# Sigmoid attention and mixture of depths on one core: sums moved from GpSimd to VectorE, small transfers moved to GpSimd, and a new order at the end

## The chip, the cores and the metric

The kernel runs on one core of a Trainium2 chip. The metric is device time in microseconds (us), the median of the runs of one kernel. The kernel before takes 510.37 us (three runs, 508.68 to 512.42).

A core has five engines, each with an instruction stream of its own: TensorE (PE in the profile; its weight loads are PEld), VectorE (DVE), ScalarE (ACT), GpSimd (POOL) and SyncE (SP), which here only issues transfers. Each works strictly in its program's order: what waits at the head of a stream holds up all that stands behind it. Transfers between HBM and the on-chip memory (SBUF) run on DMA engines. They are issued by SyncE or by GpSimd, each of which has a queue of its own. Products land in PSUM, in eight banks.

## The reference

```python
# attention: q, k, v are (8 batches, 12 heads, 448 tokens, 64), float32
scores = q @ k^T / 8 - log(448)
attn   = sigmoid(scores)
x      = attn @ v, heads side by side: (8, 448, 768)
# mixture of depths, per batch b
s      = x[b] @ w_gate                       # one score per token
top    = the 128 tokens with the largest s
h      = relu(x[b, top] @ w1)                # w1: 768 x 1024
ye     = h @ w2                              # w2: 1024 x 768
out[b] = x[b]; out[b, top] += sigmoid(s[top]) * ye
```

## The kernel before

**Attention, by stage.** A stage `s` (0 to 11) handles two groups of four heads, in seven units `n`. A unit (`unit`, L269 and L277) multiplies a block of keys with all queries and puts the sigmoid on ScalarE. The product with the values (`values`, L304) runs in four steps: step 0 at the end of its own stage, steps 1 to 3 in the first three units of the next. `take` (L319) then turns the result into rows per token on VectorE, and `gates` (L327, L330) adds up gate scores from them. Keys and queries come in by token (`load`, L100), and VectorE turns them (`turn`, L244 to L251): for stage s+1 after unit 5 of stage s, and the second half early in stage s+1. The values come by `load_v` (L119, L121) after unit 3.

**Routing, by batch.** A batch is complete after one and a half stages. `store` (L336) writes its rows to DRAM, `gate` (L348 to L363) makes the scores, `spread` (L370) brings them to all partitions by way of DRAM (L358), `rank` (L378, L381) counts how many tokens score higher, and `place` (L389 to L394) carries the ranks through DRAM into a tile `spot`. `choose` (L406 to L426) picks from it the token of each rank and its score, puts the sigmoid on that score (L421, ScalarE) and gathers the 128 rows `xe` (GpSimd, L426). `copy_out` (L339) copies all rows to the output, and `scatter` (L567, GpSimd) writes the chosen rows over them at the end.

The small transfers of this chain (scores, rep, ranks, spot) are issued by GpSimd for batches 0 and 1 (scores and rep for 7 also), and by SyncE for the others. On SyncE they stand among the large ones, and rep waits there until scores has landed, spot until ranks has.

**The two matrix products of the chosen rows** work on pairs `p` of batches, with a scheme of Strassen's kind: instead of eight products of half-size blocks there are seven, of sums of blocks. So there are sums on three sides:

- Sums of the weights, four for each matrix, made once: `load_weights` (L135 to L167). It loads four quarters of a matrix (L152), makes four 128x1536 sums on GpSimd (L166) and stores each in DRAM (L157). It is called for matrix 1 after unit 5 of stage 0, and for matrix 2 after unit 5 of stage 1. Later `lend` (L177) brings a sum back into tiles that the attention has just freed, shortly before its product.
- Sums of the turned rows: `turn_rows` transposes `xe` on TensorE (L448), ScalarE and VectorE copy it out of PSUM (L451 to L454), and three sums of 128x384 follow (L457), a fourth in `last_row` (L467). They run on VectorE for pairs 0 and 3 and on GpSimd for pairs 1 and 2.
- Sums of the hidden rows: `first` makes the seven products with matrix 1 (L484). `first_sums` adds their results on VectorE (L497) and applies relu on ScalarE (L500). After product 3 come four more sums, of hidden rows with each other: on GpSimd for pairs 0 to 2 (L532), and on VectorE for pair 3 (L522 to L527). `second` makes the seven products with matrix 2 (L546), and `second_sums` multiplies by the gate and adds to `xe` (L557).

**What sets the order.** It is written out by hand; nothing reorders it. `WORK` (L577) says after which unit of which stage each product stands, `LENT` (L589) which sums are lent in which stage, and `routed` and `gap` where the routing steps go. In `do` (L601), the sums of first product 7 are held until those of the next product have been issued. After stage 11, `rest` (L667) lists the remaining work: the last batches' routing, the pair 2 and then the pair 3.

Of the kernel before, what the change touches and what calls it, by code (L numbers as in the profile page):

```python
# [17 lines left out]
def kernel(  # L18
# [124 lines left out]
    def load_weights(m):  # L143
        n = KH if m == 1 else FH
        w = (w1_sb, w2_sb)[m - 1]
        held = [(0, 0), (0, 1), (1, 1)] if m == 1 else [(0, 0), (1, 0), (1, 1)]
        left = (1, 0) if m == 1 else (0, 1)
        room = moe.tile([P, 7 * FH * P], F32, name="hidden")
        a, b = room[:, :QW], room[:, QW:2 * QW]
        c = moe.tile([P, 6 * KH * P], F32, name="rows_t")[:, :QW]  # L150
        for dst, at in [(a, left)] + [(w[:, x], held[x]) for x in (2, 0, 1)]:
            nc.sync.dma_start(out=dst.rearrange("p (t c) -> p t c", t=n), in_=quarter(m, *at))  # L152
        w00, wx, w11 = [w[:, x] for x in range(3)]

        def made(key, src):
            t = sums[m, key] = dram.tile([P, QW], F32, name=f"sum{m}{key}", bufs=1)
            nc.gpsimd.dma_start(out=t, in_=src)  # L157

        if m == 1:
            ops = [(5, b, a, w11, ALU.add), (6, c, b, w00, ALU.subtract),  # L160
                   (7, a, w00, a, ALU.subtract), (3, b, wx, c, ALU.subtract)]
        else:
            ops = [(5, b, a, w00, ALU.subtract), (6, c, w11, b, ALU.subtract),
                   (7, a, a, w11, ALU.subtract), (4, b, wx, c, ALU.subtract)]
        for key, dst, x, y, op in ops:
            nc.gpsimd.tensor_tensor(out=dst, in0=x, in1=y, op=op)  # L166
            made(key, dst)  # L167
# [173 lines left out]
    def queue(b):  # L341

        return nc.gpsimd if b < 2 or b == B - 1 else nc.sync

    def gate(b):
# [12 lines left out]
        queue(b).dma_start(out=scores, in_=total[:TB])  # L358
# [8 lines left out]
    def spread(b):  # L367
        scores = st[b]["scores"]
        rep = st[b]["rep"] = moe.tile([P, S], F32, name="rep", bufs=2)
        queue(b).dma_start(out=rep, in_=bass.AP(tensor=scores.tensor, offset=scores.offset,  # L370
                                                ap=[[0, P], [1, S]]))
# [13 lines left out]
    def place(b):  # L385
# [5 lines left out]
        queue = nc.gpsimd if b < 2 else nc.sync  # L391
        queue.dma_start(out=ranks, in_=by_col)
        spot = moe.tile([P, 4, NC * TT], F32, name="spot")
        queue.dma_start(  # L394
# [4 lines left out]
    def choose(b):  # L399
# [15 lines left out]
        for m in range(pieces):  # L415
            at = moe.tile([P, 1], I32, name="idx", bufs=8)
# [3 lines left out]
        gt = moe.tile([P, 1], F32, name="gate", bufs=4)  # L420
        nc.scalar.activation(gt[:n], picked[1][:n], AF.Sigmoid)  # L421
# [7 lines left out]
        st[b].update(idx=idx, gate=gt, xe=xe)  # L429
# [6 lines left out]
    def turn_rows(b, where="o"):  # L436
# [13 lines left out]
        if not odd:  # L450
            nc.scalar.activation(x[:, 0:2, :, :n], ps[:, :, :KH, :n], AF.Copy)  # L451
            return
        nc.scalar.activation(x[:, 2, :, :n], ps[:, 0, :KH, :n], AF.Copy)
        nc.vector.tensor_copy(x[:, 3, :, :n], ps[:, 1, :KH, :n])  # L454
        eng = nc.vector if p in (0, NP - 1) else nc.gpsimd
        for dst, y, z in ((4, 2, 0), (2, 3, 2), (5, 3, 4)):
            eng.tensor_tensor(out=x[:, dst, :, :n], in0=x[:, y, :, :n], in1=x[:, z, :, :n],  # L457
                              op=ALU.subtract)
        pairs[p]["turned"] = eng
        last_row(p)  # L460

    def last_row(p):

        n = CAP
        if pairs[p].get("turned") and pairs[p].get("second"):
            x = pairs[p]["x"]
            pairs[p]["turned"].tensor_tensor(out=x[:, 1, :, :n], in0=x[:, 1, :, :n],  # L467
                                             in1=x[:, 5, :, :n], op=ALU.subtract)
# [22 lines left out]
    def first_sums(p, key, ps):  # L491
# [27 lines left out]
        else:  # L519
            add(h[2], ps, h[2])  # L520
            if p == NP - 1:
                nc.vector.scalar_tensor_tensor(out=h[4], in0=h[2], scalar=0.0, in1=h[3],  # L522
                                               op0=ALU.max, op1=ALU.add)
                nc.vector.tensor_tensor(out=h[5], in0=h[4], in1=h[0], op=ALU.subtract)
                nc.vector.scalar_tensor_tensor(out=h[2], in0=h[2], scalar=0.0, in1=h[0],
                                               op0=ALU.max, op1=ALU.subtract)
                nc.vector.tensor_tensor(out=h[6], in0=h[1], in1=h[5], op=ALU.subtract)  # L527
                return
            relu(h[2])
            for dst, a, b, op in ((4, 2, 3, ALU.add), (5, 4, 0, ALU.subtract),  # L530
                                  (2, 2, 0, ALU.subtract), (6, 1, 5, ALU.subtract)):
                nc.gpsimd.tensor_tensor(out=h[dst], in0=h[a], in1=h[b], op=op)  # L532
# [31 lines left out]
    def scatter(b, m=None):  # L564
# [14 lines left out]
        (5, 3): [("t", 1)], (5, 4): [(1, 0, 7), (1, 0, 6)], (5, 5): [(1, 0, 4), (1, 0, 5)],  # L579
        (6, 3): [(2, 0, 1), (2, 0, 2)], (6, 4): [(1, 0, 3)], (6, 5): [(2, 0, 4), (2, 0, 5)],  # L580
        (7, 3): [(2, 0, 3)], (7, 4): [(2, 0, 6)], (7, 5): [(2, 0, 7), ("s", 0), ("t", 2)],
        (8, 3): [("t", 3), (1, 1, 1)], (8, 4): [(1, 1, 2), (1, 1, 7)],
        (8, 5): [(1, 1, 6), (1, 1, 4)],
# [5 lines left out]
    LENT = {5: [(1, 7), (1, 6), (1, 5)], 6: [(1, 3), (2, 4), (2, 5)], 7: [(2, 6), (2, 7)],  # L589
            8: [(1, 7), (1, 6)], 9: [(1, 5), (1, 3), (2, 4)], 10: [(2, 5), (2, 6), (2, 7)],  # L590
# [10 lines left out]
    def do(item, where="o"):  # L601
# [5 lines left out]
        else:  # L607
            args = begin(item, where)
            if item[0] == 1 and item[2] == 7:
                held.append((item, args))  # L610
                return
# [160 lines left out]
```

## Time and profile before

| engine | busy us | share of the span |
|---|---|---|
| PE | 450.2 | 89% |
| PEld | 261.2 | 51% |
| DVE | 292.6 | 58% |
| ACT | 184.4 | 36% |
| POOL | 90.9 | 18% |

The profiled execution has a span of 507.7 us. TensorE is busy in 89% of it, and its clock was granted at 0.956 of full speed on average. The page's second part shows the span in 40 slices; a digit below 9 in the PE row, or in the PEclk row, marks where something else sets the pace. A row of the time order gives the start and the length in us, the engine, the line, the operation and its tiles, and in brackets how long the engine was idle ahead of it and who ended that. In a list of waits, the three numbers are the total in us, how many times, and the longest.

Some durations that are used below, each the mean of its group: a VectorE sum of 128x384 out of SBUF takes 0.55 us (L457) and of 128x512 0.69 us (L524); on GpSimd they take 1.08 us (L457) and 1.33 us (L532), and a 128x1536 weight sum takes 3.44 us (L166). Issuing a transfer on GpSimd takes 0.56 us (L157).

### The profile page before, as it was taken

What the parts mean: (1) busy time and instruction counts of PE and PEld (TensorE: products, weight loads), DVE (VectorE), ACT (ScalarE), POOL (GpSimd) and SP (SyncE); (2) the same over time, 40 slices, a digit from 0 to 9 for tenths busy, and PEclk for the clock granted to TensorE, in tenths of its full rate; (3) what the DMA queues carried; (4) which work ended last, traced back from release to release, by engine and by line L of the source; (5) the groups of instructions that cost most, each with busy time, mean ns of one, the idle gap of its engine ahead of it and who ended that gap; (6) DMA issues with size and microseconds to landing.
All of it is one profiled execution on the core that took longest, in us unless ns stands there. A gap on an engine that the chain in (4) does not pass through costs nothing. (4 is left out here: it accounts for less than half of the span.)

```text
span 507.7 us, 14392 instructions
## 1 busy us (share of the span) xinstructions
PE 450.2 (89%) x6326; PEld 261.2 (51%) x6326; DVE 292.6 (58%) x637; ACT 184.4 (36%) x240; POOL 90.9 (18%) x90
## 2 busy tenths in 40 slices
PE   8998973989998999994999899996999997927994
PEld 3553531445645745442447645543456485517952
DVE  4319197697527568664419468675427478722361
ACT  4745550555543343343353343443245201001000
POOL 8084192110000000400103000300102105001002
PEclk9999995999999999998899999998999999877998
DMA  8978997699689659695677749696549658926901
GB/s 258 344 284 240 335 257 198 199 160 316 109 276 257 112 177 261 111 282 180 135 289 197 128 158 258 112 306 214 124 157 253 108 139 163 392 97 235 312 28 46
DMA packets 134841, 104.19 MB, mean 205 GB/s; under 512 B 98124, under 2 KB 116268, under 8 KB 134524
## 3 DMA queue, kind: packets, MB, share of 16 engines
q1 hardware_dynamic: 131612, 89.35, 64.7%
q0 software_dynamic: 3168, 13.93, 8.7%
q8 instruction: 49, 0.80, 0.7%
q14 instruction: 12, 0.10, 0.1%
HBM read 82.67 MB, written 31.60 MB: 225 GB/s over the span
## 5 line engine op out<-in xcount | busy, mean ns | idle before, releaser
L269 PE MATMUL psc<-qT,kT 32*64 32x448 f32 x2496 | 150.0, 546 | 15.4 <-DVE qT L251 10.5
L304 PE MATMUL o<-attn_d,raw_v 32*64 32x448 f32 x1152 | 128.8, 536 | 1.4 <-issue 1.0
L304 PE MATMUL o<-attn_u,raw_v 32*64 32x448 f32 x1152 | 123.5, 535 | 0.8 <-ACT o L307 0.8
L277 ACT ACTIVATE attn_u<-psc,bias_s 128x896 f32<-128x896 f32 x86 | 81.9, 1004 | 94.9 <-PE psc L269 94.8
L269 PEld LDWEIGHTS psc<-qT,kT 32*64 32x64 f32 x2496 | 58.9, 132 | 80.8 <-issue 55.3
L277 ACT ACTIVATE attn_d<-psc,bias_s 128x896 f32<-128x896 f32 x70 | 66.7, 1004 | 58.6 <-PE psc L269 56.1
L319 DVE STREAM_TRANSPOSE x_b<-o 128x448 f32<-128x448 f32 x48 | 26.9, 618 | 83.4 <-PE o L304 83.4
L304 PEld LDWEIGHTS o<-attn_u,raw_v 32*64 32x64 f32 x1152 | 50.4, 132 | 31.0 <-issue 25.1
L304 PEld LDWEIGHTS o<-attn_d,raw_v 32*64 32x64 f32 x1152 | 50.6, 132 | 24.8 <-issue 21.8
L546 PE MATMUL o<-attn_d,hidden 128*128 128x384 f32 x88 | 37.1, 578 | 14.0 <-DMA attn_d<-sum 14.0
L557 DVE SCALAR_TENSOR_TENSOR xe<-o,gate,xe 128x384 f32<-128x384 f32 x40 | 22.6, 610 | 34.9 <-PE o L546 34.9
L484 PE MATMUL o<-rows_t,w_sb 128*128 128x128 f32 x216 | 28.2, 291 | 12.6 <-ACT rows_t L451 9.1
L327 DVE TENSOR_TENSOR scr<-x_b,wg_b 128x448 f32<-128x448 f32 x48 | 38.3, 798 | 1.0
L532 POOL TENSOR_TENSOR hidden<-hidden 128x512 f32<-128x512 f32 x12 | 15.8, 1334 | 112.2 <-ACT hidden L500 111.9
L484 PE MATMUL o<-rows_t,attn_d 128*128 128x128 f32 x288 | 34.5, 277 | 1.2 <-DVE rows_t L457 1.2
L484 PEld LDWEIGHTS o<-rows_t,attn_d 128*128 128x128 f32 x288 | 33.0, 192 | 4.8 <-DVE rows_t L457 2.0
L484 PEld LDWEIGHTS o<-rows_t,w_sb 128*128 128x128 f32 x216 | 26.7, 204 | 16.8 <-ACT rows_t L451 9.4
L546 PEld LDWEIGHTS o<-attn_d,hidden 128*128 128x128 f32 x88 | 19.0, 223 | 30.9 <-issue 22.4
L497 DVE TENSOR_TENSOR hidden<-o,hidden 128x512 f32<-128x512 f32 x24 | 15.9, 687 | 31.5 <-PE o L484 31.3
L500 ACT ACTIVATE hidden<-hidden 128x512 f32<-128x512 f32 x15 | 9.4, 630 | 59.3 <-DVE hidden L497 59.3
L330 DVE TENSOR_REDUCE gate_p<-scr 128x14 f32<-128x448 f32 x48 | 29.8, 621 | 1.7
L378 DVE TENSOR_SCALAR_CACHE_REDUCE scr<-rep,score 128x448 f32<-128x448 f32 (+1 forms) x32 | 21.5, 672 | 11.4 <-DMA rep<-scores 10.6
(108 smaller groups left out, 449.7 us busy)
## 6 DMA issues: line engine op xcount, KB each, us to landing
attn_d<-sum SPq DMA_DIRECT2D x56, 384.0 KB, 7.5
x_d<-x_b SPq DMA_DIRECT2D x32, 336.0 KB, 7.2
out_dram<-x_d SPq DMA_DIRECT2D x8, 1344.0 KB, 9.8
raw_k<-in_k_dram SPq DMA_DIRECT2D x23, 448.0 KB, 8.4
raw_q<-in_q_dram SPq DMA_DIRECT2D x23, 448.0 KB, 5.0
raw_v<-in_v_dram SPq DMA_DIRECT2D x48, 192.0 KB, 8.9
w_sb<-in_moe_w_dram SPq DMA_DIRECT2D x6, 768.0 KB, 12.5
sum<-hidden POOLq DMA_DIRECT2D x6, 768.0 KB, 6.8
```

Source lines behind the costliest of these rows:

```text
L269: nc.tensor.matmul(psc[h // 2][y * Dh:(y + 1) * Dh, h % 2, :S], kT[2 * s + x][d, e, r:r + 2, :].rearrange("d r t -> d (r t)"), qT[2 * s + ...
L277: nc.scalar.activation(a, psc[pr][:, :, :S], AF.Sigmoid, bias=bias_s, scale=QK_SCALE)
L304: nc.tensor.matmul(o[x][j * Dh:(j + 1) * Dh, pr, :S], w, a[rows, j, :], start=(n == 0 and c == 0), stop=(n == 3 and c == NF - 1))
L319: nc.vector.transpose(x_tiles[b][:, :, 2 * g + pr, :], outs[s][x][:, pr, :S].rearrange("p (r t) -> p r t", t=TT))
L327: nc.vector.tensor_tensor(out=tmp, in0=x_tiles[b][:, :, hp, :], in1=wg_b[:, hp:hp + 1, :].to_broadcast([P, TB, TT]), op=ALU.mult)
L330: nc.vector.tensor_reduce(out=gate_parts[b][:, :, hp], in_=tmp, axis=AX.X, op=ALU.add)
L378: nc.vector.tensor_scalar(out=junk[:n], in0=rep[:n], scalar1=own, scalar2=0.0, op0=ALU.is_gt, op1=ALU.add, accum_out=above[:n, c:c + 1])
L484: nc.tensor.matmul(ps[:, f, :n], w((t * FH + f) * P, P), x[:, t, :n], start=(t == 0), stop=(t == KH - 1))
L497: nc.vector.tensor_tensor(out=dst, in0=a, in1=b, op=ALU.add)
L532: nc.gpsimd.tensor_tensor(out=h[dst], in0=h[a], in1=h[b], op=op)
L546: nc.tensor.matmul(ps[:n, :DH], h[:, t, :n], w(t * DH, DH), start=(t == 0), stop=(t == FH - 1))
L557: nc.vector.scalar_tensor_tensor(out=xe[:n, cols], in0=ps[:n, :DH], scalar=st[b]["gate"][:n, 0:1], in1=xe[:n, cols], op0=ALU.mult, op1=ALU ...
```

## The change

It has six parts.

- **Weight sums.** `load_weights` is split. After unit 5 of stage 0, one quarter and three held quarters of matrix 1 are loaded and its four sums made on GpSimd as before; the three held quarters of matrix 2 are loaded in the same place. The remaining quarter of matrix 2 is loaded in stage 1 after unit 1, into the buffer that held matrix 1's, and its four sums are made on VectorE after unit 4 of stage 1. The held quarters are now loaded in the order 0, 1, 2 instead of 2, 0, 1.
- **Small transfers.** Scores, rep, ranks and spot are issued by GpSimd for all batches, so that SyncE carries only the large ones.
- **Other sums.** The sums of turned rows (L457, L467) and of hidden rows (L532) go to VectorE for all pairs; for two of the hidden sums relu is taken into the sum instead of standing on ScalarE. The turned rows' sums come in the order 4, 5, 2 instead of 4, 2, 5.
- **Products 6 and 7.** First product 6 stands ahead of 7, and nothing is held back any more.
- **The gate's sigmoid** moves from `choose` to `turn_rows`, behind the copy of the turned rows.
- **The end.** In `rest`, three sums are lent ahead of the last batch's store, more are lent early, batch 6 is chosen before the last ranking, and the four hidden sums are spread between products and ranking, so that second products 2, 4, 1 and 5 start before batch 7's ranking is done.

```diff
-    def load_weights(m):
...
-        for dst, at in [(a, left)] + [(w[:, x], held[x]) for x in (2, 0, 1)]:
-            nc.sync.dma_start(out=dst.rearrange("p (t c) -> p t c", t=n), in_=quarter(m, *at))
...
+    def load_held(m):
+        for x, at in enumerate((HELD1, HELD2)[m - 1]):
+            load_quarter(m, (w1_sb, w2_sb)[m - 1][:, x], at)
+    def load_left(m):
+        if m == 1:
+            t = moe.tile([P, 7 * FH * P], F32, name="hidden")
+            room["a"], room["b"] = t[:, :QW], t[:, QW:2 * QW]
+        load_quarter(m, room["a"], (1, 0) if m == 1 else (0, 1))
+    def make_sums(m, eng):
...
         for key, dst, x, y, op in ops:
-            nc.gpsimd.tensor_tensor(out=dst, in0=x, in1=y, op=op)
-            made(key, dst)
+            eng.tensor_tensor(out=dst, in0=x, in1=y, op=op)
+            t = sums[m, key] = dram.tile([P, QW], F32, name=f"sum{m}{key}", bufs=1)
+            nc.gpsimd.dma_start(out=t, in_=dst)
...
-        queue(b).dma_start(out=scores, in_=total[:TB])
+        nc.gpsimd.dma_start(out=scores, in_=total[:TB])
...
-        queue.dma_start(out=ranks, in_=by_col)
+        nc.gpsimd.dma_start(out=ranks, in_=by_col)
...
-        gt = moe.tile([P, 1], F32, name="gate", bufs=4)
-        nc.scalar.activation(gt[:n], picked[1][:n], AF.Sigmoid)
...
         if not odd:
             nc.scalar.activation(x[:, 0:2, :, :n], ps[:, :, :KH, :n], AF.Copy)
...
+        st[b]["gate"] = moe.tile([P, 1], F32, name="gate", bufs=4)
+        nc.scalar.activation(st[b]["gate"][:n], st[b]["picked"][:n], AF.Sigmoid)
...
-        eng = nc.vector if p in (0, NP - 1) else nc.gpsimd
-        for dst, y, z in ((4, 2, 0), (2, 3, 2), (5, 3, 4)):
+        for dst, y, z in ((4, 2, 0), (5, 3, 4), (2, 3, 2)):
+            nc.vector.tensor_tensor(out=x[:, dst, :, :n], in0=x[:, y, :, :n],
+                                    in1=x[:, z, :, :n], op=ALU.subtract)
...
-                nc.gpsimd.tensor_tensor(out=h[dst], in0=h[a], in1=h[b], op=op)
+            for m in sums_too:
+                hidden_sum(p, m)
...
-        (5, 3): [("t", 1)], (5, 4): [(1, 0, 7), (1, 0, 6)], (5, 5): [(1, 0, 4), (1, 0, 5)],
+        (5, 3): [("t", 1)], (5, 4): [(1, 0, 6), (1, 0, 7)], (5, 5): [(1, 0, 4), (1, 0, 5)],
...
-        (8, 3): [("t", 3), (1, 1, 1)], (8, 4): [(1, 1, 2), (1, 1, 7)],
-        (8, 5): [(1, 1, 6), (1, 1, 4)],
+        (8, 3): [("t", 3), (1, 1, 1)], (8, 4): [(1, 1, 2), (1, 1, 6)],
+        (8, 5): [(1, 1, 7), (1, 1, 4)],
...
-        lend(1, 3, "d10")
+        for key, slot in (((1, 3), "d10"), ((2, 4), "d11"), ((2, 5), "d12")):
+            lend(*key, slot)
         work = [(item, begin(item, "any")) for item in ((1, p, 6), (1, p, 7))]
...
-        for key in (4, 5, 3):
+        for key in (4, 5):
             do((1, p, key), "any")
+        first_sums(*begin((1, p, 3), "any"), sums_too=())
...
+        choose(b - 1)
+        work = [((2, p, key), begin((2, p, key), "any")) for key in (2, 4, 1)]
+        hidden_sum(p, 5)
+        work.append(((2, p, 5), begin((2, p, 5), "any")))
         ranking(b)
...
+        work = [((2, p, key), begin((2, p, key), "any")) for key in (6, 7)]
...
         choose(b)
...
-                if n == NU - 2 and s < 2:
-                    load_weights(s + 1)
+                if (s, n) == (0, NU - 2):
+                    load_left(1)
+                    load_held(1)
+                    make_sums(1, nc.gpsimd)
+                    load_held(2)
+                elif (s, n) == (1, 1):
+                    load_left(2)
+                elif (s, n) == (1, 4):
+                    make_sums(2, nc.vector)
```

## The prediction

> **What bounds the kernel now.** I read the page's busy shares first (PE 89%, VectorE 58%, ScalarE 36%, GpSimd 18%), then TensorE's list of waits, then the time order of each engine around every wait over 2 us. TensorE works through one fixed order; what isn't matmul there is a few long waits. Its list of waits (us in total, times, longest):
>
> ```profile
> PE o L546 <- DMA attn_d<-sum: 14.0, 3, 6.6
> PE psc L269 <- DVE qT L251: 10.5, 2, 9.6
> PE o L484 <- ACT rows_t L451: 9.1, 1, 9.1
> PE o L484 <- DVE hidden L497: 3.1, 2, 2.2
> PE psc L484 <- DVE rows_t L457: 2.9, 1, 2.9
> ```
>
> In order of time these are the gaps that matter (the bracket is the idle time ahead of the row):
>
> ```profile
> 84.56 3.29 PE L269 MATMUL psc<-qT,kT 32*64 32x448 f32 x32 [9.56 <-DVE qT L251]
> ...
> 239.52 5.45 PE L546 MATMUL o<-attn_d,hidden 128*128 128x384 f32 x8 [6.61 <-DMA attn_d<-sum]
> ...
> 286.48 2.92 PE L484 MATMUL o<-rows_t,w_sb 128*128 128x128 f32 x24 [2.20 <-DVE hidden L497]
> ...
> 352.01 8.10 PE L546 MATMUL o<-attn_d,hidden 128*128 128x384 f32 x16 [4.48 <-DMA attn_d<-sum]
> ...
> 455.92 4.81 PE L484 MATMUL o<-rows_t,w_sb 128*128 128x128 f32 x24 [9.14 <-ACT rows_t L451]
> 466.96 4.43 PE L484 MATMUL psc<-rows_t,attn_u 128*128 128x128 f32 x24 [2.89 <-DVE rows_t L457]
> ```
>
> A gap costs more than itself. In the busy table by stretch the granted clock is 0.53 for 84.5 to 88.0, 0.52 for 239.5 to 245.0 and 0.50 for 352.0 to 357.5, and 1.00 just after each. Half of such a stretch is lost: 1.6, 2.6 and 2.75 us.
>
> Why each arises. **At 84.56** VectorE's own time order shows the cause, beside GpSimd's:
>
> ```profile
> 66.50 3.65 DVE L327 TENSOR_TENSOR scr<-x_b,wg_b 128x448 f32<-128x448 f32 x1
> 71.43 6.91 DVE L353 COPY parts<-by_dim 32x32 f32<-32x32 f32 x4
> 70.53 3.45 POOL L166 TENSOR_TENSOR hidden<-hidden,w_sb 128x1536 f32<-128x1536 f32 x1
> 74.87 3.43 POOL L166 TENSOR_TENSOR hidden<-w_sb,rows_t 128x1536 f32<-128x1536 f32 x1
> ```
>
> The same rows take 0.63 and 0.72 us when GpSimd is silent. VectorE is held up while GpSimd makes the second matrix's sums (61.9 to 78.3), and the turn of the next queries queues behind.
>
> **At 239.52** the lent weights come late. SyncE's order:
>
> ```profile
> 231.63 0.38 SPq L394 DMA_DIRECT2D spot<-ranks  x1
> 232.14 3.59 SPq L177 DMA_DIRECT2D attn_d<-sum  x4
> ```
>
> The values product that frees the lent tiles ended at 226.7, but SyncE stood from 223.5 to 231.6 waiting for ranks to land, so lending began 5.4 us late, behind spot's own transfer. 352.01 is the same: L394 at 344.7, values done at 341.4.
>
> **At 455.92** the turned rows were in PSUM at 446.8, but ScalarE stood in front of them:
>
> ```profile
> 454.97 0.20 ACT L421 ACTIVATE gate<-got 128x1 f32<-128x1 f32 x1 [18.01 <-DVE scr L406]
> 455.08 0.79 ACT L451 ACTIVATE rows_t<-psc 128x768 f32<-128x768 f32 x1
> ```
>
> **What the skill says.** *SBUF — State Buffer*, "SBUF: two separate sides": VectorE and GpSimd share a port pair as an exclusive lock, held for a whole instruction, where VectorE has two SBUF inputs or a fast mode. The trace agrees (3.65 against 0.63 us). *TensorE: Matmul & The Clock Gate*, "What's actually happening": the clock is half or full, halved after an idle window of about 3.4 us. The trace agrees (0.50 to 0.53 after the three long gaps). *DMA: Bandwidth & Descriptors*, "Queues, rings and completion order": each engine consumes a ring in order, and other rings take turns with it. The landings agree: the four first-weight quarters landed at 23.6, 26.4, 28.4 and 30.4, as issued; gate rows that GpSimd issued by 4.1 landed by 10.0, ahead of SyncE loads issued at 2.6 and 3.1 (10.5 and 12.3). No page prices the waits below; I use the trace's rows.
>
> **Part 1, the second matrix's sums on VectorE.** Removed: four 3.44 us GpSimd sums. Added: four VectorE sums of 128x1536. No such row exists; 128x384 takes 0.55 and 128x512 0.69, so 1.09 us per 1000 elements: 0.69 + 1024 x 0.00109 = 1.8, four are 7.2 (bounds 1.7 and 2.0 each). They stand ahead of the turn for stage 2, so they are on TensorE's path, and so is a new wait. The left quarter of matrix 2 goes into the buffer of matrix 1's left quarter; SyncE waits there for sum 7 of matrix 1 to be stored. Working it through:
> - GpSimd's first sum needs held quarter (1,1), now third in the queue: it lands at 30.4 instead of 26.4, so the sums start at 30.5 instead of 26.5. In the trace sum 7's store was issued 12.5 us after the start: 43.1. Stores take 4.2 to 6.9 us to land; the other traffic is queued behind, so 4.3: 47.4.
> - The quarter is issued then. A 448 KB load issued at 47.98 landed in 3.4 us; with 768 KB and sum 3's store beside it, 5 to 6.5: it lands at 52.5 to 54.
> - Queued behind it on SyncE are stage 1's values (L119, L121), in place at 46.3 before. Now four of about 1 us each follow the quarter: 57. TensorE wants them at 44.3 and stands.
> - VectorE starts at 53.5; the fourth sum overwrites what sum 5's store reads, issued at 55.6, landing 4.2 to 6.9 us later (60 to 62.5). Then 1.8 for that sum and 2.3 for the turn (L244, L246, L251): queries at 63.2 to 67.3, I take 65.3. TensorE's stage 2 began at 49.1: **16.2 us late**.
> - What comes back: stage 2 took 25.9 us to the 9.56 gap. VectorE now runs undisturbed: values turned 12.5 us into the stage, then 12.2 us of work to the next queries (98.63 to 110.85 in stage 3) fits the 25.9. So the gap goes, -9.6; half clock after the new gap costs 1.6 to 2.75 against 1.6 before: +0.6. Net **+7.2** (4.5 to 9.7).
>
> **Part 2, small transfers on GpSimd.** SyncE no longer stands for scores (2.6 us ahead of each store of rows) or ranks. Lending starts when the values product ends (226.8, 341.6), behind raw loads that end at 231.4 less about 3 us of earlier row stores. The weights land by 232, wanted at 232.9 and 347.5. Gains 6.6 + 2.6 and 4.5 + 2.75 = **-16.4** (to -12 if a microsecond or two stays in each). GpSimd's route is slower (ranks 3.3 to 6.0 us, spot 6.2 to 9.0), hidden: the choice from it is a whole stage later. GpSimd's queued scatters wait for VectorE as before.
>
> **Part 3, product 6 ahead of 7 and GpSimd's other sums to VectorE.** In stage 8, 7's sums are held until 6's, and the next product waits 2.2 us for the bank. In the new order 6's sum runs beside the scores: **-2.0**. The hidden sums become 0.69 on VectorE for 1.33 on GpSimd, the row sums 0.55 for 1.08; TensorE waited for none of them, and they come earlier: 0. Row order 4, 5, 2: product 6 needs row 5, the second made, as product 7 needed row 2, the second made: 0.
>
> **Part 4, the end.** TensorE starts at 409.1 as before: five first products (13.9), then second 2, 4, 1, 5 at 2.6 each to 433.5; their weights are now lent ahead of the row stores, so the 2.96 wait at 431.3 goes. VectorE: first sums to 424.4, choice for batch 6 1.5, sum 5 0.7, then ranking 6.1 from about 426.8 (the copies of scores land at 426.3 in both): done at 433.1. Before, the ranks then stood in SyncE's queue until 440.2. On GpSimd: ranks land at 436.5 to 438, spot 4 to 6 us after: 440 to 444. TensorE goes on with 6, 7, 3 and turned rows until 443.2. First product 1 needs 6's bank, free after choice (1.5) and three sums (1.8): 443.4 to 447; with product 2 and the second turned rows (2.7 + 2.7 + 0.8) 449.7 to 453.3, up to 455.5 at half clock, against 464.1 before. The sigmoid stands behind the copied rows, so it stops nobody. From there the order is the same. **-11** (-8.5 to -14.4).
>
> Sum: 7.2 - 16.4 - 2 - 11 = -22.2. Against the median 510.4: about **488.5**.
>
> **Rivals.** *The waits move only in part* (17%): earlier lending meets raw loads and values in the same ring (for it: the DMA engines are 0.78 and 0.80 busy from 207 to 241 and from 320 to 360), and the last choice stays late; half of parts 2 and 4: 510.4 + 7.2 - 8 - 2 - 5.5 = 502. Against: landings follow issue at once when SyncE is free. *The front costs nothing* (15%): the store lands soon and the end goes best: 510.4 - 16.4 - 2 - 14 = 478. Against: TensorE wants the values at 44.3, before the store can land. *Slower* (8%): the 16.2 stays in full with a second gap at stage 3 (VectorE has only 1 us of slack), +17; parts 2 and 4 give only 4 and 2, part 3 2: 519. Against: half the old stage-2 gap is lock time that surely goes.
>
> **Chances.** The forecast 60%. Best ends together: 4.5 - 16.4 - 2 - 14.4 = -28.3, 482; worst together 9.7 - 12 - 1.5 - 8.5 = -12.3, 498. Reaching a little to the neighbours: 480 to 500. Faster by over 1% (under 505.3) 0.90, within 1% 0.04, slower 0.06.
>
> **What would show it.** Right: TensorE waits about 12 us at 45 for raw_v and some 5 at 60 for qT, no gap at the start of stage 3; no wait for lent weights in stages 7 and 10; ScalarE's L451 row directly after the transposes; the second turned rows 9 to 14 us earlier relative to stage 12. Wrong: values in place at 50 or earlier; SyncE idle but weights still late; a new wait of TensorE for VectorE in the middle; stage 12 waiting for the gather of batch 7.

## The result, and the profile after

The changed kernel takes **492.51 us** (median of 4 runs, 491.7 to 496.88); the kernel before took 509.52 beside it (4 runs, 508.68 to 512.42). The ratio is 0.9674, with a 95% interval of 0.9603 to 0.9745. Forecast were 488.5, range 480 to 500. The gain is 17.0 us, where the sum of the steps was 22.2. (All ratios here leave disturbed runs out, so one can differ a little from the quotient of two medians.)

The profiled executions are 491.2 us after and 507.7 before. The busy shares of the page after:

```profile
PE 448.8 (91%) x6326; PEld 276.1 (56%) x6326; DVE 300.2 (61%) x661; ACT 181.7 (37%) x237; POOL 66.5 (14%) x88
```

GpSimd lost 24 us of work and VectorE gained 8, but TensorE does the same work as before. So the gain has to be in TensorE's waits. Its list of waits after (us in total, times, longest):

```profile
PE o L314 <- DMA raw_v<-in_v_dram: 9.6, 2, 8.8
PE o L490 <- DVE xe L566: 8.4, 1, 8.4
PE psc L279 <- ACT attn_u L287: 4.9, 6, 1.4
PE psc L490 <- issue: 2.9, 1, 2.9
PE psc L279 <- DVE qT L261: 1.9, 1, 1.9
```

None of the three large waits of before is left: not the lent weights (14.0), not the rows behind the sigmoid (9.1), and the wait for turned queries is 1.9 instead of 10.5. Two new ones stand there, for the values (9.6) and for a PSUM bank (8.4; a product can't start until VectorE's sums have emptied the bank that it writes to). TensorE's order of time shows where:

```profile
53.78 1.75 PE L314 MATMUL o<-attn_d,raw_v 32*64 32x448 f32 x4 [8.85 <-DMA raw_v<-in_v_dram]
56.32 1.76 PE L314 MATMUL o<-attn_d,raw_v 32*64 32x448 f32 x4 [0.79 <-DMA raw_v<-in_v_dram]
...
65.58 2.85 PE L279 MATMUL psc<-qT,kT 32*64 32x448 f32 x32 [1.93 <-DVE qT L261]
...
437.72 4.75 PE L490 MATMUL o<-rows_t,w_sb 128*128 128x128 f32 x24 [8.38 <-DVE xe L566]
...
448.74 4.38 PE L490 MATMUL psc<-rows_t,attn_d 128*128 128x128 f32 x24 [2.93 <-issue]
```

I account by milestones: the first score matmul of each stage, the first matmul of the rest, and the second turned rows of the end (445.0 after, 463.2 before). All numbers are after minus before, from the profiled executions:

| stretch | measured | forecast |
|---|---|---|
| start to stage 2 | +16.5 | +16.2 |
| stages 2 and 3 | -10.5 | -9.0 |
| stage 5 | -1.9 | 0 |
| stage 7 | -9.0 | -9.2 |
| stage 8 | -2.2 | -2.0 |
| stage 10 | -6.9 | -7.2 |
| the rest, to the second turned rows | -4.5 | -11 |
| from there to the end | +1.8 | 0 |

With 0.2 in the other stages that is -16.5. One row is far off, the one up to the second turned rows, by 6.5 us. Stage 5 and the last stretch, for which the prediction had no term, are off by 1.9 and 1.8; that these two cancel is chance.

### The profile page after: what moved, and what is told of

It is laid out like the page before. It is cut to its first block, busy times and chain, and to the rows that moved or that the text cites. A ratio compares the mean times of both kernels' runs of the same rounds, so it can differ in the third digit from the quotient of the medians.

```text
span 491.2 us, 14384 instructions
## 1 busy us (share of the span) xinstructions
PE 448.8 (91%) x6326; PEld 276.1 (56%) x6326; DVE 300.2 (61%) x661; ACT 181.7 (37%) x237; POOL 66.5 (14%) x88
## 4 chain that ended last, share of the span: by engine, by line
PE 71%; DVE 8%; DMA 8%; issue 5%; POOL 3%; ACT 1%; SPq 1%; POOLq 0%; DVEq 0%; ACTq 0%
PE o L314 24%; PE psc L279 21%; PE o L490 11%; PE o L555 9%; PE psc L490 3%; DMA w_sb<-in_moe_w_dram 3%; POOL hidden L175 2%; PE o L279 2%; DMA spot<-ranks 2%; DVE x_b L329 2%; ACT attn_u L287 1%; DVE gate_p L340 1%; DMA ranks<-by_col 1%; DVE scr L337 1%; PE psc L555 1%
## 5 line engine op out<-in xcount | busy, mean ns | idle before, releaser
L279 PE MATMUL psc<-qT,kT 32*64 32x448 f32 x2496 | 152.3, 544 | 6.9 <-ACT attn_u L287 4.9
L314 PE MATMUL o<-attn_d,raw_v 32*64 32x448 f32 x1152 | 134.3, 547 | 10.0 <-DMA raw_v<-in_v_dram 9.6
L314 PE MATMUL o<-attn_u,raw_v 32*64 32x448 f32 x1152 | 129.3, 544 | 0.8 <-ACT o L317 0.8
L279 PEld LDWEIGHTS psc<-qT,kT 32*64 32x64 f32 x2496 | 64.6, 131 | 65.0 <-issue 40.2
L314 PEld LDWEIGHTS o<-attn_d,raw_v 32*64 32x64 f32 x1152 | 54.1, 134 | 33.3 <-issue 16.9
L314 PEld LDWEIGHTS o<-attn_u,raw_v 32*64 32x64 f32 x1152 | 56.4, 134 | 27.5 <-issue 18.3
L503 DVE TENSOR_TENSOR hidden<-o,hidden 128x512 f32<-128x512 f32 x25 | 16.5, 686 | 20.6 <-PE o L490 20.2
L314 PE MATMUL o<-attn_u,raw_h 32*64 32x448 f32 x384 | 28.8, 551 | 0.0
L254 DVE STREAM_TRANSPOSE kT<-raw_k 128x384 f32<-128x384 f32 x46 | 23.5, 549 | 7.8 <-DMA raw_k<-in_k_dram 4.2
L555 PE MATMUL o<-attn_d,hidden 128*128 128x384 f32 x80 | 27.6, 493 | 0.0
L555 PE MATMUL o<-w_sb,hidden 128*128 128x384 f32 x80 | 27.5, 491 | 0.0
```

The lines of the kernel that those rows point to most:

```text
L254: nc.vector.transpose(kT[i][:, e, :HK], sk[:, e, :HK].rearrange("p (m c) d -> p c m d", c=NF))
L279: nc.tensor.matmul(psc[h // 2][y * Dh:(y + 1) * Dh, h % 2, :S], kT[2 * s + x][d, e, r:r + 2, :].rearrange("d r t -> d (r t)"), qT[2 * s + ...
L314: nc.tensor.matmul(o[x][j * Dh:(j + 1) * Dh, pr, :S], w, a[rows, j, :], start=(n == 0 and c == 0), stop=(n == 3 and c == NF - 1))
L503: nc.vector.tensor_tensor(out=dst, in0=a, in1=b, op=ALU.add)
L555: nc.tensor.matmul(ps[:n, :DH], h[:, t, :n], w(t * DH, DH), start=(t == 0), stop=(t == FH - 1))
```

## Experiments

The kernel before, run beside these on the same chips, had medians of 509.8 to 513.3. The first three experiments are parts of the change put into the kernel before, the next four are edits of the changed kernel, the last five test what these left open.

| kernel | median us | ratio to before, 95% |
|---|---|---|
| the change | 492.51 | 0.9674 [0.9603, 0.9745] |
| e1, part 2 alone | 488.85 | 0.9591 [0.9505, 0.9677] |
| e2, part 1 alone | 515.81 | 1.0104 [1.0036, 1.0173] |
| e3, sigmoid alone | 507.57 | 0.9938 [0.9906, 0.9971] |
| e4, values first | 494.75 | 0.9714 [0.9651, 0.9776] |
| e5, sums later | 486.3 | 0.9532 [0.9452, 0.9611] |
| e6, choice last | 490.53 | 0.9612 [0.9544, 0.968] |
| e7, ScalarE issues the last ranks | 488.98 | 0.9607 [0.9537, 0.9677] |
| e8, e5 + e6 + e7 | 480.72 | 0.9405 [0.9323, 0.9486] |
| e9, sums back on GpSimd | 493.88 | 0.9629 [0.9551, 0.9707] |
| e10, e8 and sums spread | 479.86 | 0.9375 [0.9293, 0.9457] |
| e11, e6 + e7 with the old front | 484.42 | 0.9459 [0.9384, 0.9535] |
| e12, the best | 475.12 | 0.9311 [0.923, 0.9393] |

**e1: part 2 alone, in the kernel before.**

```diff
-        return nc.gpsimd if b < 2 or b == B - 1 else nc.sync
+        return nc.gpsimd
...
-        queue = nc.gpsimd if b < 2 else nc.sync
+        queue = nc.gpsimd
```

> The kernel before, with part 2 alone: scores, rep, ranks and spot of all batches are issued by GpSimd. Theory (SyncE stood in front of the lent weights): the waits at stages 7 and 10 and their half clock go, stage 7 falls from 39.9 to about 31 us and stage 10 from 39.8 to about 33, total about 16 us less than before: 493 to 495. Rival (the lent weights wait for their turn in the ring, whoever issues the small ones): at most 4 to 8 us less, 502 to 506. The end should hardly move, because ScalarE's sigmoid still stands in front of the turned rows.

Measured: 488.85, better than either theory, and better than the whole change by its median, though the intervals overlap. Its profile has stages 7 and 10 at 30.8 and 32.6 us (39.9 and 39.8 before; 31.0 and 32.9 in the changed kernel), so the mechanism of part 2 is right. What nobody forecast is that the end is 6.6 us shorter too, 47.5 us from the start of the rest to the second turned rows instead of 54.1. The order of time of GpSimd, VectorE and ScalarE in e1:

```profile
418.57 0.57 POOL L392 DMA_DIRECT2D ranks<-by_col  x1 [5.57 <-DVE by_col L389]
...
424.01 0.75 POOL L394 DMA_DIRECT2D spot<-ranks  x1 [4.88 <-DVE xe L557]
...
429.64 0.68 DVE L406 SCALAR_TENSOR_TENSOR scr<-spot,slot,number 128x448 f32<-128x448 f32 x1 [3.91 <-DMA spot<-ranks]
...
431.10 0.20 ACT L421 ACTIVATE gate<-got 128x1 f32<-128x1 f32 x1 [9.18 <-DVE scr L406]
431.64 0.81 ACT L451 ACTIVATE rows_t<-psc 128x768 f32<-128x768 f32 x1 [0.34 <-PE psc L448]
```

Before, the last ranks stood in SyncE's queue behind lent weights until 440.20 and spot until 448.71. With both on GpSimd the last choice comes 37.6 us into the rest instead of 44.4, and the sigmoid, still in its old place, has left ScalarE before the turned rows arrive. So the sigmoid wait, which I had given to part 4, goes with part 2 as well. The gap of 9.4 at the start of stage 3 is still there, as it has to be without part 1.

**e2: part 1 alone, in the kernel before** (the functions and the calls of the changed kernel's weight loading).

> The kernel before, with part 1 alone: the second matrix's sums on VectorE, its left quarter loaded in stage 1 after unit 1. Theory (a new wait at the front that is longer than the one removed): stage 2 begins at about 65.5 instead of 49, stage 3 begins without a gap; 5 to 7 us more than before: 514 to 517. Rival (the lock between VectorE and GpSimd was the loss, and it goes): 9 to 11 us less, 499 to 501.

Measured: 515.81, a loss of 1.0% (interval 0.4 to 1.7), as expected. TensorE's order of time in e2 has the front of the changed kernel:

```profile
53.00 1.76 PE L314 MATMUL o<-attn_d,raw_v 32*64 32x448 f32 x4 [6.54 <-DMA raw_v<-in_v_dram]
...
64.86 3.01 PE L279 MATMUL psc<-qT,kT 32*64 32x448 f32 x32 [2.02 <-DVE qT L261]
```

Stage 3 starts at 91.3, against 84.6 before, without a gap there. Moving the second matrix's sums as it was done costs about 5 us; the change gains in spite of its part 1.

**e3: the sigmoid behind the turned rows, alone, in the kernel before.**

```diff
-        gt = moe.tile([P, 1], F32, name="gate", bufs=4)
-        nc.scalar.activation(gt[:n], picked[1][:n], AF.Sigmoid)
...
+        st[b]["gate"] = moe.tile([P, 1], F32, name="gate", bufs=4)
+        nc.scalar.activation(st[b]["gate"][:n], st[b]["picked"][:n], AF.Sigmoid)
```

> The kernel before, with the gate's sigmoid moved behind the copy of the turned rows and nothing else. Theory (the wait behind the sigmoid hides another: the second turned rows wait for batch 7's gather, which landed at 459.6): the 9.1 us gap goes, but a new one of 4 to 5 us appears at the second turned rows, 3 to 5 us less than before: 505 to 507. Rival (the sigmoid was the whole cause): 8 to 9 us less, 500 to 502.

Measured: 507.57. Of the 9.1 us wait, 3.7 come back as time (50.4 us to the second turned rows instead of 54.1). (The runs give 3 to 4 in all. This profile, with a span of 510.0, can't be used for the total: the waits for lent weights, which this edit leaves alone, are 20.0 us in it instead of 14.0.) In TensorE's order of time the next wait stands behind it, for the gather of batch 7, which needs the same late choice:

```profile
453.75 2.94 PE L486 MATMUL o<-rows_t,w_sb 128*128 128x128 f32 x24 [0.96 <-ACT rows_t L449]
465.31 1.51 PE L446 MATMUL o<-iden,attn_u 128*128 128x128 f32 x6 [5.94 <-DMA attn_u<-x_d,row]
```

**e4: the left quarter of matrix 2 loaded later, so that stage 1's values go first.**

```diff
-                elif (s, n) == (1, 1):
+                elif (s, n) == (1, 3):
                     load_left(2)
```

> The changed kernel, with the left quarter of matrix 2 loaded after unit 3 of stage 1, behind that stage's values instead of ahead of them. Theory (two waits in series: values behind the quarter, then queries behind the sums on VectorE): TensorE no longer waits for values at 45, but stage 2 still begins at 64 to 68, because the sums and the turn still wait for the quarter; total as the changed kernel, 490 to 495. Rival (the wait for values is the whole loss): the 8.85 us come back, 483 to 485.

Measured: 494.75, with an interval that overlaps that of the change. The wait for the values is gone, and one of 16.0 us for turned queries stands in its place; stage 2 starts at 64.8 instead of 65.6. The list of waits in e4:

```profile
PE psc L279 <- DVE qT L261: 16.0, 1, 16.0
PE o L490 <- DVE xe L566: 6.6, 1, 6.6
```

The two waits of the front are in series: taking away the first only moves it to the second. Both stand behind the late quarter, as e5 shows.

**e5: quarter and sums later still.**

```diff
-                elif (s, n) == (1, 1):
+                elif (s, n) == (1, 5):
                     load_left(2)
-                elif (s, n) == (1, 4):
+                elif (s, n) == (2, 1):
                     make_sums(2, nc.vector)
```

> The changed kernel, with the left quarter loaded after unit 5 of stage 1 and the four sums on VectorE after unit 1 of stage 2, where VectorE stood idle for 12 us. Theory (the loss at the front is the place of the load and of the sums, not the sums on VectorE): stage 2 begins at 49 to 50 and stage 3 at 75 to 77, 15 to 17 us less than the changed kernel: 475 to 478. Rival (VectorE has too little room in stage 2, so that the 7 us of sums come out at stage 3): 8 to 10 us less, 482 to 485.

Measured: 486.3. The theory missed, and it is a microsecond beyond the rival's range too. Stage 2 starts at 52.7 and stage 3 at 81.9 instead of 92.0, so the position of the quarter and of its sums was worth 10 us there, of which 6.2 are left in the medians. Not all 16 came back. VectorE's order of time in e5 shows one reason:

```profile
44.85 3.62 DVE L337 TENSOR_TENSOR scr<-x_b,wg_b 128x448 f32<-128x448 f32 x1
49.16 0.63 DVE L337 TENSOR_TENSOR scr<-x_b,wg_b 128x448 f32<-128x448 f32 x1
...
51.51 1.07 DVE L261 STREAM_TRANSPOSE qT<-raw_q 128x896 f32<-128x896 f32 x1
```

GpSimd still makes the first matrix's sums until 48, and VectorE is held for 3.6 us in an instruction of 0.63 (the exclusive port pair of the Trainium skill, *SBUF — State Buffer*, "SBUF: two separate sides"). In the kernel before these sums began at 26.5; in e5 they begin at 31.5, as the held quarter (1,1) now lands third of the held ones, and so they reach into the time of the turn.

**e6: the last choice behind the sums of second products 6, 7 and 3.**

```diff
-        choose(b)
         for item, args in work:
             finish(item, args)
         do((2, p, 3), "any")
+        choose(b)
```

> The changed kernel, with batch 7's choice on VectorE behind the sums of second products 6, 7 and 3 instead of ahead of them. Theory (the 8.4 us wait at the end is a bank held by sums that stand behind the choice): the next products start right after the turned rows, and the second turned rows then wait for batch 7's gather, 2 to 4 us less than the changed kernel: 488 to 491. Rival (the bank is the whole wait): 8 us and the half clock less, 483 to 485.

Measured: 490.53. The bank wait is gone, so its cause is shown: the sums that free the bank stood behind the choice on VectorE. 5.4 us of it return as a wait for the gather: the second turned rows come 46.2 us into the rest, 3.5 earlier. Of these, 1.5 are lost again behind them, where the clock stays at half for 10.2 us (442.2 to 452.5) instead of 3.4, and the intervals of e6 and the change overlap. TensorE's order of time in e6:

```profile
431.56 2.95 PE L490 MATMUL o<-rows_t,w_sb 128*128 128x128 f32 x24 [0.90 <-ACT rows_t L454]
...
442.56 1.51 PE L451 MATMUL o<-iden,attn_u 128*128 128x128 f32 x6 [5.37 <-DMA attn_u<-x_d,row]
```

**e7: ScalarE issues ranks and spot of the last batch.**

```diff
-        nc.gpsimd.dma_start(out=ranks, in_=by_col)
+        eng = nc.scalar if b == B - 1 else nc.gpsimd
+        eng.dma_start(out=ranks, in_=by_col)
...
-        nc.gpsimd.dma_start(
+        eng.dma_start(
             out=spot, in_=bass.AP(tensor=ranks.tensor, offset=ranks.offset,
```

> The changed kernel, with ranks and spot of batch 7 alone issued by ScalarE instead of GpSimd. Theory (GpSimd's route is slow while the lent sums fill the DMA engines: 6.2 and 7.8 us): ranks and spot take about 9 us together instead of 15, so 4 to 7 us less than the changed kernel: 485 to 489. Rival (the DMA engines are full, whoever issues): spot lands as late as before, 491 to 494.

Measured: 488.98, 3.5 us less by the medians, with intervals that overlap; second turned rows 42.9 us after the start of the rest instead of 49.7 (in this profile 1.7 us are lost before the rest begins, mostly in stages 4 and 5, which the edit leaves alone). The issues of ScalarE and the choice of VectorE in e7:

```profile
421.07 0.36 ACTq L398 DMA_DIRECT2D ranks<-by_col  x1
424.18 0.38 ACTq L400 DMA_DIRECT2D spot<-ranks  x1
...
429.37 0.68 DVE L412 SCALAR_TENSOR_TENSOR scr<-spot,slot,number 128x448 f32<-128x448 f32 x1 [2.16 <-DMA spot<-ranks]
```

From the first issue to the choice: 8.3 us, against 14.6 in the changed kernel (419.83 to 434.39). This shows that these two transfers set the pace up to the second turned rows. It doesn't show that GpSimd's route as such is slow. In e7 SyncE's own list of waits has something new, and its lent weights stop:

```profile
SPq L187 <- DMA ranks<-by_col: 6.1, 1, 6.1
SPq L187 <- DMA spot<-ranks: 5.0, 1, 5.0
```

In the busy table by stretch the DMA engines are 0.64 and 0.48 busy while the two travel in e7; in the changed kernel they are 1.02 and 1.01 busy. A cleared road and another queue came together. Why SyncE waits there can be read from the semaphores in the trace: the transfers of SyncE and ScalarE take eight semaphores of the program in turn, and a transfer that takes one waits until the transfer before it on that semaphore has landed. Ranks and spot had taken the next two, so SyncE's next lends were issued at 424.07 and 429.41, just as these two landed. It is the program that cleared the road here.

**e8: e5, e6 and e7 together.**

> The changed kernel with three earlier edits together: the left quarter of matrix 2 loaded after unit 5 of stage 1 and its sums after unit 1 of stage 2; the last batch's ranks and spot issued by ScalarE; the last choice behind the sums of second products 6, 7 and 3. If the front and the end are independent: 486.3 less the end's saving (the last bank wait gone with no gather wait in its place, since spot lands earlier), 481 to 484; second turned rows 42 to 43.5 us after the rest begins. Rival: with the choice last, the gather of batch 7 is late whatever issues ranks and spot, and a wait for it of 3 us or more stands there: 485 to 487.

Measured: 480.72, just under the range of the first theory: front and end are independent to about a microsecond (the rest starts at 385.8, at 386.7 in e5). A gather wait of 3.2 does stay, as the rival had it, but the second turned rows come at 43.8, only 0.3 later than the theory's range.

**e9: the row sums of pairs 1 and 2 and the hidden sums of pairs 0 and 1 back on GpSimd,** in the changed kernel, with its order of products.

> The changed kernel with the row sums of pairs 1 and 2 and the hidden sums of pairs 0 and 1 back on GpSimd (the order of the products stays). If moving them to VectorE was worth nothing, as forecast: 491 to 494, stages 3 to 10 within 1 us of the changed kernel each. Rival: on GpSimd they hold VectorE by the shared port and stand ahead of the small transfers, which are now all issued there: stages 5, 6, 8 and 9 longer by 1 to 3 us each, 496 to 502.

Measured: 493.88. Stages 4 to 10 are within 0.6 us of the changed kernel each, stage 3 is 1.1 longer and stage 2 0.9 shorter. The 0 for moving these sums holds, as far as they were moved back (pair 2's hidden sums stay on VectorE). Stage 8 is 37.5 here (37.1 changed, 39.3 before, 39.9 in e1, 40.0 in e2 and e3), so by elimination its gain is the order of 6 and 7 with nothing held back; no run has this part alone.

**e10: as e8, all eight weight sums on VectorE, one at a time between units.**

```diff
+                    one = make_sums(1, nc.vector)
+                elif s == 1 and n in (2, 3, 4, 5):
+                    next(one)
+                    if n == 5:
+                        load_left(2)
+                        one = make_sums(2, nc.vector)
+                elif s == 2 and n in (1, 2, 3, 4):
+                    next(one)
```

> As the run with all three edits, and the first matrix's four sums on VectorE as well, one after each of the units 2 to 5 of stage 1, the second's one after each of the units 1 to 4 of stage 2. If GpSimd's sums holding VectorE are what stage 1 still lost, and a sum between two units hides: stage 2 starts at 49 to 51 and stage 3 at 76 to 79 instead of 81.9, 476 to 481 in all. Rival: VectorE has no room in stages 1 and 2, its 14 us of sums reach TensorE in full or the left quarter comes later than unit 1: stage 3 at 82 or later, 482 to 486.

Measured: 479.86; stage 2 starts at 50.3 (52.1 in e8), as the theory had it, stage 3 at 80.0, a microsecond later than it had. The last two sums, at 74.30 and 75.97, stood ahead of the turn of stage 3's queries, and TensorE waited 4.5 there. Against e8 the gain in all is inside the intervals.

**e11: e6 and e7 with the weight loading of the kernel before.**

> The changed kernel without part 1 (both matrices' weights loaded and summed as in the kernel before, on GpSimd), with ScalarE issuing the last ranks and spot and the last choice behind the sums. The changed kernel lost 7.4 us to the start of stage 3 (92.0 against 84.6); the end gains 3 to 4: 480 to 483. Rival: parts 2 and 4 lean on the new front (VectorE freed in stage 2), and without it waits come back in stages 2 and 3: 486 or more.

Measured: 484.42, just above the range of the theory. Stage 3 starts at 84.8, so no new wait appears in stages 2 and 3, and parts 2 and 4 don't lean on part 1; stage 10 is 1.2 us longer than in the changed kernel. Next to it e5's front, in e8, starts stage 3 at 82.4: placed well, part 1 is a gain of 2 us, placed as in the change a loss of 7.

**e12: as e10, the last choice ahead again, and the sums so placed that more turns go first.**

```diff
-                elif s == 1 and n in (2, 3, 4, 5):
+                elif s == 1 and n in (1, 2, 3, 5):
...
-                elif s == 2 and n in (1, 2, 3, 4):
+                elif (s, n) in ((2, 2), (2, 3), (2, 5), (3, 1)):
```

> As the run with the sums spread over stages 1 and 2, with two edits: the last choice again ahead of the sums of second products 6, 7 and 3 (with ScalarE issuing ranks and spot that left a 1.85 us bank wait and no gather wait: 42.9 us from the rest's start to the second turned rows against 45.5), and each sum one unit earlier or later so that the turns go first: matrix 1 after units 1, 2, 3 and 5 of stage 1, matrix 2 after units 2, 3 and 5 of stage 2 and unit 1 of stage 3. Theory: the end gains 1 to 3, the front 1 to 3 (no wait at the start of stage 2, a smaller one in stage 2): 474 to 478. Rival: the sums only move their cost into the next turn, and the gains at both ends are under 1: 478.5 to 481.

Measured: **475.12**, faster than both kernels (its interval ends at 0.9393, that of the change begins at 0.9603). Stage 3 starts at 76.3, and the second turned rows come 43.7 us into the rest. Its list of waits:

```profile
PE psc L280 <- ACT attn_u L288: 4.9, 6, 1.4
PE psc L280 <- DVE qT L262: 2.9, 1, 2.9
PE psc L492 <- issue: 2.7, 1, 2.7
PE o L492 <- DVE xe L568: 2.2, 1, 2.2
```

No single wait of 3 us is left in it. The one of 2.9 is at the start of stage 3, where one sum (at 72.30) still stands ahead of the turn. Against e8 and e10 the intervals overlap; what the two edits gained each was not run.

## Why the prediction was right, and where it was off

**The front, +7.2 forecast, +6.0 measured to the start of stage 4.** The chain of events held, with one link missed. VectorE's order of time after:

```profile
55.86 1.76 DVE L175 TENSOR_TENSOR hidden<-hidden,w_sb 128x1536 f32<-128x1536 f32 x1 [5.23 <-DMA sum<-hidden]
57.66 1.76 DVE L175 TENSOR_TENSOR rows_t<-w_sb,hidden 128x1536 f32<-128x1536 f32 x1
59.33 1.75 DVE L175 TENSOR_TENSOR hidden<-hidden,w_sb 128x1536 f32<-128x1536 f32 x1
61.54 1.76 DVE L175 TENSOR_TENSOR hidden<-w_sb,rows_t 128x1536 f32<-128x1536 f32 x1 [0.46 <-DVE hidden L175]
```

Sum 7's store landed at 47.7 (forecast 47.4), the values at 58.2 (57), a sum takes 1.76 us (1.8), and stage 2 starts at 65.58 (65.3). VectorE began 2.4 us later than forecast, since it waited for the store of sum 3, which I had not counted as its releaser, but the slack before the last sum took that up. (The range in the text for the queries, 63.2 to 67.3, is wider than its terms give, 64.1 to 66.6; the middle is the same.) The split on TensorE differs: 9.6 us of waits for values and 1.9 for queries, where I had 12 and 5, since TensorE started at 53.8 with the first of the four value loads. The other loss between 49 and 63 is half clock. In the busy table by stretch, after (stretch, sum, busy of PE, PEld, DVE, ACT and POOL, then the granted clock):

```profile
49.10:62.80 13.70, 8.23 (x62) 3.08 (x64) 7.91 (x7) 0.00 (x0) 1.60 (x3) 0.50 0.90 288
434.80:441.70 6.90, 3.98 (x19) 4.01 (x20) 4.41 (x13) 0.00 (x0) 2.01 (x2) 0.51 0.95 378
```

The Trainium skill's *TensorE: Matmul & The Clock Gate*, "What's actually happening", says that the clock is halved after an idle window; here it stays so for some 9 us after the 8.85 us wait, against 3 to 5.5 us after the other long waits of the two traces, with a second short wait inside (0.79, at 55.5). That stages 2 and 3 give back 10.5 instead of 9.0 is the gap gone, as forecast, and 1.5 in stage 3.

**Part 2 in stages 7 and 10, -16.4 forecast, -15.8 measured.** The lent weights are in time: no wait for them in the list, and SyncE issues them when the values product ends. SyncE in stage 7, after:

```profile
229.89 2.50 SPq L187 DMA_DIRECT2D attn_d<-sum  x4
```

The product that needs them starts at 237.2 without a wait. e1 shows the same with part 2 alone. But the term was drawn too small around those two stages: e1 also shortens the end by 6.6 us and stage 5 by 1.6 of the change's 1.9 (37.3 us, 38.9 before, 37.0 after); how it does so in stage 5, I have not shown. One reading in this part doesn't fit the trace of before: "GpSimd's route is slower" doesn't hold there for ranks (8.5 and 6.4 us on SyncE in the two cases with a landing, 3.3 and 6.0 on GpSimd).

**Part 3, -2.0 forecast, -2.2 measured,** with e9 for the 0 of the moved sums and, by elimination, for the order.

**The end, -11 forecast, -4.5 measured: the step that was mis-sized.** The ranking is done 24.2 us into the rest, where the working put it (433.1 less 409.1, 24.0). Then it says "ranks land at 436.5 to 438, spot 4 to 6 us after", 7.4 to 10.9 us in all. GpSimd's issues, VectorE's choice, and the chain of waits, after:

```profile
419.83 0.56 POOL L397 DMA_DIRECT2D ranks<-by_col  x1 [6.14 <-DVE by_col L395]
426.55 0.76 POOL L399 DMA_DIRECT2D spot<-ranks  x1 [6.16 <-DMA attn_d<-sum]
...
434.39 0.68 DVE L411 SCALAR_TENSOR_TENSOR scr<-spot,slot,number 128x448 f32<-128x448 f32 x1 [8.69 <-DMA spot<-ranks]
```

```profile
419.83 6.17 DMA ranks<-by_col
426.55 7.82 DMA spot<-ranks
437.72 4.75 PE o L490 x24
```

From ranking done to spot landed: 14.8 us (6.2 for ranks, 7.8 for spot, the issues between). The 4 to 6 for spot contradict my own text, which gives 6.2 to 9.0 for spot on GpSimd in part 2, from the trace of before, and there calls it hidden. At the end it isn't. After, the seven spots whose landing the trace has take 7.0 to 8.7. With 6.0 and 7.6, the upper ranks time and the median for spot on GpSimd before, the step had come out at 14 us. So the term that failed is the time of ranks and spot at the end, 14.8 us where the working had 7.4 to 10.9, and with it the sign that the second turned rows would come 9 to 14 us earlier. The choice, and with it the three sums that free the bank, came 4 to 8 us later than the working had them, TensorE stood 8.4 us and then ran some 4 us at half clock (the second line of the stretches above). e6 and e7 show both halves: take the choice from in front of the sums and the bank wait goes; make the two transfers faster and nearly all of it goes (1.85 left), with 6.8 us.

The comparison with e1 is sharper. Part 2 alone brings the second turned rows at 47.5 us into the rest, the whole change at 49.7. So the new order of the end, as written, brought nothing on top of part 2; in that order the choice stands ahead of the sums, and the slow transfer reaches TensorE through the bank instead of through ScalarE. The order did bring the ranking forward, from 26.2 us into the rest in e1 to 24.2. But in e1 spot has landed 11.3 us after the ranking and in the changed kernel 14.8, both on GpSimd's queue. While spot travels, SyncE issues no lent sum in e1 (the last at 419.3) and six in the changed kernel, where part 4 lends more at this time; the DMA engines are 0.84 and 1.01 busy. That the lends slow spot down fits all this, and e7 too, but no run changes the lends alone.

**The last stretch, 0 forecast, +1.8 measured.** To the issue of the last scatter both kernels need 39.4 us. From there to the end it is 5.1 us before and 6.9 after (502.60 and 484.34 to 507.7 and 491.2). It is 5.1 to 5.2 in e2 and e3, which leave the small transfers alone, and 6.7 to 6.9 in e1 and in all nine others. So it comes with part 2. The last scatter lands after 2.6 us in both; what grows is a DRAIN instruction of GpSimd at the end of the program (before, after and e7; of the three times in ns the third, the longest, is the one):

```profile
L767 POOLq DRAIN  x3: 46/97/4537, 502.4 to 507.4; - x3
...
L789 POOLq DRAIN  x3: 46/97/6333, 484.1 to 491.0; - x3
...
L790 POOLq DRAIN  x3: 46/97/6170, 479.0 to 485.7; - x3
```

GpSimd issues 40 transfers before, 62 after and 60 in e7, so each one more adds 0.08 us at the end; the other runs have one of these three counts and its time. This small price of part 2 I had put at nothing.

**The rivals.** "The waits move only in part" came true for the end and not for stages 7 and 10. "The front costs nothing" fell: it cost 6. "Slower" fell with the gap of stage 3. Taken together: the signs of all four terms held, and the mechanisms of the first three; for the end the mechanism held (choice, three sums, bank) and a size failed. The order of the end without part 2 was not run. (The sum of the terms gives 488.2, where the text says about 488.5.) -22.2 became -16.5 in the profiles by +6.5 at the end, +1.8 behind it and +0.6 in stages 7 and 10, less 1.9 in stage 5 and 1.2 at the front. What stage 5 gave back is luck.

## What to carry to other kernels

When a transfer moves to another queue, look up its time on that queue wherever it is on the path, not only where it is hidden, and look for every instruction that queues behind its arrival; at the end of a kernel nothing hides it. An edit that removes a wait in the middle may free the end as well: run the parts alone, since here one of four brought as much as all together, and another cost 5 us. Sums that must be made somewhere can hide one at a time between units of work, each behind whatever the bounding engine waits for next: in e10 two stood ahead of the turn for stage 3 and TensorE waited 4.5 us, in e12 one does and it waits 2.9.

## What the runs showed that I had not expected

- The transfer of the same 256 KB spot takes 7.0 to 8.7 us on GpSimd's queue in the changed kernel, 5.2 on ScalarE's in e7 and 4.8 on SyncE's before (448.71 to 453.51). The last two ran on less loaded DMA engines (0.48 and 0.22 busy), so queue and load are not fully told apart; but in e1, with the engines 0.84 busy, GpSimd's took 5.6, so the queue alone doesn't make it slow.
- Each transfer that GpSimd issues, wherever it stands, costs 0.08 us at the very end: kernels in which it issues all or nearly all small transfers end 1.6 to 1.8 us later after their last scatter, in all ten experiments of this kind.
- Half clock comes in steps. In the two traces it lasts 10.25, 6.83, 6.83, 3.41, 10.24 and 3.41 us before, and 13.65, 3.41, 6.82 and 3.41 after (leaving out the last one, which runs into the end): each time one to four steps of 3.41 (the busy table by stretch gives 0.50 for each). So the price of a wait jumps with where it falls among the steps: a step more is half of 3.41, up to 1.7 us. Behind the second turned rows in e6 it is two steps more than in the change, and 1.5 us.
- Four VectorE sums of 128x1536 take 1.76 us each against 3.44 to 3.45 on GpSimd, and one at a time they can cost TensorE little (e12: stage 2 starts at 48.4 and stage 3 at 76.3, 49.1 and 84.6 before). In e5, with matrix 2's four in a row, stage 3 starts at 81.9, though there GpSimd still makes matrix 1's sums; the two are not told apart.
